# Strided attention of seven batches, two residue classes at a time on the array's rows

## The chip, the cores and the metric

The kernel runs on one core of a Trainium2 chip. The metric is the device time of one execution in microseconds (us). TensorE (PE) multiplies matrices, PEld is its loading of weights, VectorE is DVE, ScalarE is ACT, GpSimd is POOL, and SyncE (SP) issues transfers. All five work from queues of their own, each in the order written, and wait for one another by semaphores.

## The reference

The inputs are q, k and v, each 8 batches x 8 heads x 576 positions x 64 elements. Heads 0 to 3 attend locally, heads 4 to 7 with a stride of 32. The output of attention goes through a two-layer network whose activation is the square of a ReLU.

```python
rel = pos[:, None] - pos[None, :]
mask_local = (rel >= 0) & (rel < 32)
mask_strided = (rel >= 0) & (pos[None, :] % 32 == pos[:, None] % 32)
scores = where(mask, q @ k.T / 8, -1e9)          # mask_local for h < 4, else mask_strided
x = softmax(scores) @ v                          # to 4608 tokens x 512
out = square(maximum(x @ w_in, 0)) @ w_out       # 512 -> 2048 -> 512
```

In a strided head a position attends only to positions of its own residue class modulo 32. There are 32 classes of 18 positions in each head.

## The kernel before, in words

Tokens pass through the network in nine chunks of 512. `mm1(c, ff)` makes one of 16 blocks of the hidden layer of chunk c: four matmuls of 128x512 (L604), a ReLU on ScalarE into one of four `r` buffers (L610), and a square on VectorE into `g_sb` (L611). `mm2` makes the output rows, four such matmuls a group (L626), and ScalarE copies a finished bank out (L630). So the whole run is 288 groups of four wide matmuls each, 32 groups for a chunk: 16 of mm1, then 16 of mm2. Bank `ph` has two buffers.

Attention is woven between these groups. A batch is four units of two heads; units 4b and 4b+1 are local, 4b+2 and 4b+3 strided. Batch 0 comes first (the string `BATCH0`), since chunk 0 needs it. For the others the string `PLAN` gives, for each group number, the words that are run ahead of that group; the numbers are called steps below. What a word issues stands in that order in the queue of each engine it uses, so a late instruction holds up whatever is written behind it on its engine. Work that was put off with `later` is issued at the end of a step. Attention tiles use five PSUM banks named `pt` in rotation.

The words that matter here:

| word | what it does |
|---|---|
| `l`, `c`, `T` | load local q or k rows, cast them into order (`c12kv`: unit 12, k, on VectorE; `a` is ScalarE), transpose them by TensorE (`T12ka`) and copy the result out |
| `r`, `W` | load strided q or k of batch 1 as rows, transpose them by TensorE |
| `C`, `X` | load strided q or k of later batches, transpose them by a transfer of SP |
| `Q`, `Y` | the same for local units of later batches |
| `V`, `U` | load v of the local heads, of the strided heads |
| `o` | load a quarter of `w_out` |
| `S` | scores of a unit, exponentials, masks (the masks come one to four steps later); with `!` the exponentials are issued at once |
| `D`, `E` | local: times v, division, transposition into `xt` |
| `B` | spread a strided unit's v into `vs`, beside columns of ones |
| `F` | strided: times v, one half (`F6.1`: unit 6, odd residues) |
| `z` | constants, at step 0 |

Strided attention before: 72 partitions hold 4 residue classes of 18 positions, so a unit has 8 blocks of 72x72 scores for each of its two heads. `step_S` computes them with 16 matmuls that use half of the array's rows each (one head on rows 0 to 63, the other on 64 to 127, L452), four exponentials of 72x288 (L462) and two masks (L468). `step_X` multiplies by v with 8 matmuls for each half, whose 128 weight columns are v and ones, so that sums come out beside the products (L562). Then come two logarithms (L563), an exponential of minus that (L564), and two multiplications on VectorE that write every second token of `xt` (L567).

Transfers of GpSimd go through one queue of transfers, which is served in order. Eight of them can be under way: before each further one GpSimd waits for the one eight places back. A transfer's descriptors are written when GpSimd issues it.

Of the kernel before, what the change touches and what calls it, by code (L numbers as in the profile page):

```python
# [8 lines left out]
FP32 = mybir.dt.float32  # L9
# [9 lines left out]
    c0qv c0ka T0qa c1kg w2 T0kv S0 c1qv W0k0a w3 W0q0v W0k1a W0q1v T1qv w2 T1kv S2 S1 H0v D0.0 D0.1 S3  # L19
# [4 lines left out]
1: r1q U1  # L24
3: o0
4: r1k c4kv V1 c5qv
5: o1 l2k8+9 c4qv U2
6: o2 o3 V2 C2q
7: C2k
10: l2q8+9 W1q0v T4qa T4kv c5ka T5qa  # L30
12: S4
13: T5ka
14: W1q1v B7v
16: W1k0a S5!
17: W1k1a
18: D4.0
19: S6!
20: D4.1
21: D5.0
22: B6v l3k12+13 S7!  # L40
23: D5.1
24: E5v F7.0
26: X2k l3q12+13
27: E4v F6.0 c9kv
28: F6.1 V3
29: F7.1 c8qv
30: c8ka c9qv
31: X2q
32: U3
# [6 lines left out]
44: S9! D8.0  # L56
46: D8.1
47: E8
48: D9.0 Q16k S10
49: B10v  # L60
50: Q17q Q16q
51: S11! D9.1
52: Q17k
54: F10.0 X3q
55: E9 X3k C4k F10.1 C4q
56: c12qa c13qa
57: c12kv T12ka
58: c13kv B11v V4 T13qv T12qa
59: T13ka
60: F11.0  # L70
61: F11.1
# [3 lines left out]
66: Y17  # L75
67: Y16 D12.1 S13! X4k C5q
68: C5k
71: S14! E12 Q20k Q21q Q20q
72: Q21k
73: D13.0 D13.1  # L80
75: E13 B14v
77: S15
80: F14.0
83: F14.1
86: B15v
89: F15.0
91: S16!
93: F15.1
# [7 lines left out]
103: C6q S18  # L96
104: Y21
105: D17.0
106: Q25k
108: S19 D17.1  # L100
109: Q24k Q24q
111: E17
113: B18v
116: F18.0
119: F18.1
124: V6
125: B19v F19.0 F19.1
# [4 lines left out]
135: E20 X6q S22! C7q Q28k  # L112
137: C7k Q28q Y25 S23
138: D21.0
139: Q29k Q29q D21.1
142: E21
146: B23a B22v
148: F22.0
149: F22.1
151: F23.0  # L120
155: S24!
156: V7 F23.1
# [3 lines left out]
165: S26 D24.1  # L126
167: X7q
171: X7k
172: B26v
173: Y28  # L130
174: E24 D25.0 D25.1
175: F26.0 Y29
178: E25
179: S27!
180: B27v
182: F27.0
186: F26.1 F27.1
191: S28!
192: S29
197: S30!  # L140
198: D28.0
199: D29.0 B30v
200: D28.1 E28
202: S31
204: D29.1
206: E29
209: F30.0
212: B31a
213: F30.1
216: F31.0  # L150
219: F31.1
# [3 lines left out]
def kernel(  # L155
# [9 lines left out]
    nc = tc.nc  # L165
# [13 lines left out]
    SR = 80  # L179

    singles = ctx.enter_context(tc.tile_pool(name="singles", bufs=1))
    qk_st = ctx.enter_context(tc.tile_pool(name="qk_st", bufs=1))
    qk_in = ctx.enter_context(tc.tile_pool(name="qk_in", bufs=4))
    qkT = ctx.enter_context(tc.tile_pool(name="qkT", bufs=4))
    v_st = ctx.enter_context(tc.tile_pool(name="v_st", bufs=2))
# [8 lines left out]
    strT = ctx.enter_context(tc.tile_pool(name="strT", bufs=2))  # L194
# [28 lines left out]
    vss = [singles.tile([SP_, NJ, 3, D], BF16, name=f"vs{i}") for i in range(NV)]  # L223
    str_rows_t = {nm: singles.tile([SR, 4, NJ * D], BF16, name=f"{nm}_t") for nm in "qk"}
# [24 lines left out]
    def load_qk_hw(u):  # L249
        b, p = units[u]  # L250
        s = st.setdefault(u, {})
        for name, src in (("q", q), ("k", k)):
            t = qk_st.tile([QL, 2, 6 * D], FP32, name=f"{name}_st")
            nc.sync.dma_start(out=t, in_=src[b, 2 * p:2 * p + 2].rearrange("h (p j) d -> p h (j d)", j=6))
            s[name + "f"] = t
# [31 lines left out]
    def load_str_rows(b, name):  # L287
        src = q if name == "q" else k
        if b == 0:
            c = 4 if name == "q" else 8  # L290
            t = w_out_b[0:QL, c:c + NP3, :]
        else:
            t = xt[1 if name == "q" else 2][0:QL, T - NP3 * 512:T].rearrange("p (s c) -> p s c", s=NP3)
        nc.gpsimd.dma_start(out=t, in_=src[b, 4:8].rearrange("h (p j) d -> (h p) (j d)", j=NJ)
                            .rearrange("(s p) c -> p s c", p=QL))
        str_rows[b, name] = t

    def step_TS(b, name, g, copy):
        src = str_rows[b, name]
        pt = bank("pt").bitcast(BF16)[:, 0:S]  # L300
        for i in range(2):
            for s3 in range(NP3):
                c = 128 * (2 * g + i)
                o = S // 2 * i + QL * s3
                nc.tensor.transpose(pt[:, o:o + QL], src[:, s3, c:c + 128], ident[0:QL, 0:QL])  # L305
        if g == 0:
            o = strT.tile([128, 2 * NJ * SR], BF16, name=f"{name}T_s")
            str_T[b, name] = o[:, 0:2 * NJ * SP_].rearrange("c (a r) -> c a r", a=NJ // 2)
        o = str_T[b, name]
        copy(o[:, 2 * g:2 * g + 2, :].rearrange("c a r -> c (a r)"), pt)  # L310
        if g == 1:
            for i in range(2):
                st.setdefault(4 * b + 2 + i, {})[name + "T"] = \
                    o[:, :, 2 * SP_ * i:2 * SP_ * (i + 1)].rearrange("c a (h p) -> c h a p", h=2)
# [5 lines left out]
    def load_str_tall(b, name):  # L320
        src = q if name == "q" else k
        t = str_rows_t[name]
        nc.gpsimd.dma_start(out=t[0:SP_], in_=src[b, 4:8].rearrange("h (p j) d -> p h (j d)", j=NJ))  # L323
        big[b, name] = t

    def transpose_str(b, name):
        o = strT.tile([128, 2 * NJ * SR], BF16, name=f"{name}T_s").rearrange("c (n p) -> c n p", p=SR)
        nc.sync.dma_start_transpose(out=o, in_=big.pop((b, name)).rearrange("p h c -> p (h c)"))
        for i in range(2):
            st.setdefault(4 * b + 2 + i, {})[name + "T"] = \  # L330
                o[:, NJ * i:NJ * (i + 1), 0:SP_].rearrange("c (h a) p -> c h a p", h=2)
# [16 lines left out]

    def load_v_str(b):
        t = v_st.tile([SP_, 4, NJ * D], BF16, name="v_st")  # L350
        nc.gpsimd.dma_start(out=t, in_=v[b, 4:8].rearrange("h (p j) d -> p h (j d)", j=NJ))
        for i in range(2):
            st.setdefault(4 * b + 2 + i, {})["vf"] = t[:, 2 * i:2 * i + 2]

    def spread_v_str(u, copy):
        t = vss[v_slot(u)]
        copy(t[:, :, 0:3:2, :], st[u]["vf"].rearrange("p h (j d) -> p j h d", d=D))
        st[u]["v"] = t
# [127 lines left out]

    def load_v0():
        load_v_local_sw(0)
        nc.gpsimd.dma_start(
            out=vs0.rearrange("p u n d -> p (u n d)").rearrange("p (h c) -> p h c", h=4),  # L490
            in_=v[0, 4:8].rearrange("h (p j) d -> p h (j d)", j=NJ))
# [56 lines left out]

    def step_X(u, part):
        run_due(lambda x: x[1] == u)  # L550
        e = st[u]["e"]
        b, p = units[u]
        hw, vt = S // 2, st[u]["v"].rearrange("p j k d -> p j (k d)")
        rv = rv_pool.tile([128, hw], FP32, name="rv")
        pos = []
        for h in range(2):
            po = bank("pt")
            pos.append(po)
            for t in range(NJ // 2):
                w = vt[:, 2 * t + part, D * h:D * (h + 2)]  # L560
                c = S * part + hw * h + SP_ * t
                nc.tensor.matmul(po[:, SP_ * t:SP_ * (t + 1)], w, e[0:SP_, c:c + SP_], start=True, stop=True)  # L562
            nc.scalar.activation(rv[64 * h:64 * h + 64], po[64 - 64 * h:128 - 64 * h, 0:hw], AF.Ln)  # L563
        nc.scalar.activation(rv, rv, AF.Exp, scale=-1.0)  # L564
        for h in range(2):
            r = slice(64 * h, 64 * h + 64)
            nc.vector.tensor_tensor(  # L567
                xt[p][r, b * S:(b + 1) * S].rearrange("c (p j r) -> c p j r", j=NJ // 2, r=2)[:, :, :, part],
                pos[h][r, 0:hw].rearrange("c (j p) -> c p j", p=SP_),
                rv[r].rearrange("c (j p) -> c p j", p=SP_), op=ALU.mult)  # L570
        if part:
            st.pop(u)
# [97 lines left out]
    def run_step(word):  # L670
# [15 lines left out]
        elif op == "F":  # L686
            step_X(int(arg[:-2]), int(arg[-1]))
# [5 lines left out]
        elif op == "P":  # L693
            first_part([int(x) for x in arg])
        elif op == "H":
            shift_v_local(int(arg[:-1]), ENG[arg[-1]])
        elif op == "C":
            load_str_tall(int(arg[:-1]), arg[-1])
        elif op == "Q":
            load_qk_rows(int(arg[:-1]), arg[-1])  # L700
        elif op == "X":
            transpose_str(int(arg[:-1]), arg[-1])
        elif op == "Y":
            transpose_local(int(arg))
        elif op == "V":
            load_v_local_all(int(arg))
        elif op == "U":
            load_v_str(int(arg))
        elif op == "B":
            spread_v_str(int(arg[:-1]), ENG[arg[-1]])  # L710
        elif op == "l":
            load_qk_local_sw(int(arg[0]), [int(x) for x in arg[2:].split("+")], arg[1])
        elif op == "r":
            load_str_rows(int(arg[0]), arg[1])
        elif op == "i":
            load_w_in(int(arg))
        elif op == "o":
            load_w_out(int(arg))
        elif op == "z":
            late_constants()  # L720
        else:
            raise ValueError(word)

    def late_constants():
        nc.vector.tensor_copy(mask_all, mask_loc.to_broadcast([128, NL, QL]))
        nc.vector.memset(mask_all[0:32, 0], 0.0)
        for t in str_rows_t.values():
            nc.vector.memset(t[64:SR], 0.0)
        for t in kTl[2:]:
            nc.vector.memset(t[:, 0:32], 0.0)  # L730
        for t in vss:
            nc.vector.memset(t[:, :, 1, :], 1.0)  # L732
        for i, e in enumerate(es):
            if i > 1:
                nc.vector.memset(e[:, 2 * S:1280], 1.0)
# [112 lines left out]
```

## Time and profile before

| | |
|---|---|
| time of three runs | 311.53, 311.87 (median), 313.56 us |
| span of the profiled execution, first to last instruction | 309.8 us |
| PE, PEld busy | 297.7, 147.1 us |
| DVE, ACT, POOL busy | 165.1, 195.6, 65.7 us |
| wide matmuls of mm1 and mm2, from start to start | 0.216 us |
| stretch of batch 0, up to the steady groups | 22.9 us |
| mean transfer rate | 120 GB/s |

The profile is of one execution, and its page gives the span alone, not that execution's own device time. The three times are of other executions of the same program. Busy times overlap. A matmul's record ends when its result is written, so the next one starts before; costs on TensorE are therefore read from start to start.

### The profile page before, as it was taken

The numbers are of one execution on the slowest core, as the hardware profiler recorded it, in microseconds if no ns is written. First come the engines' busy times: TensorE is split into PE (matmuls) and PEld (weight loads), VectorE is DVE, ScalarE is ACT, GpSimd is POOL, SyncE is SP. The second block draws the span as 40 slices with busy tenths as digits, with TensorE's granted clock in tenths as the row PEclk, the third lists the DMA queues.
The fourth block names the chain that finished last, engine by engine and source line by source line (L and its number), as shares of the span: only waits on it lengthen the run. The fifth ranks groups of instructions, "written<-read, shape, count | busy, mean of one in ns | idle before, by whom it ended". The sixth has DMA issues, their size and how long they took to land.

```text
span 309.8 us, 5985 instructions
## 1 busy us (share of the span) xinstructions
PE 297.7 (96%) x2288; PEld 147.1 (47%) x2288; DVE 165.1 (53%) x388; ACT 195.6 (63%) x421; POOL 65.7 (21%) x90
## 2 busy tenths in 40 slices
PE   7987999999899999999999999999999999999996
PEld 2543555445454444444545454445454544444444
DVE  4568765767647763664367554763586334203400
ACT  3774955876877775675488676865777656316611
POOL 8834422006230026047100740000000000000000
PEclk9999999999999999999999999999999999999999
DMA  8999999997999999799996999711101110010012
GB/s 152 190 204 205 190 197 182 156 156 112 177 161 166 142 124 173 161 118 112 161 205 116 119 176 198 136 24 70 68 2 38 68 70 1 34 68 36 0 67 71
DMA packets 97820, 37.23 MB, mean 120 GB/s; under 512 B 78848, under 2 KB 93312, under 8 KB 97792
## 3 DMA queue, kind: packets, MB, share of 16 engines
q0 software_dynamic: 59136, 18.76, 60.0%
q1 hardware_dynamic: 38512, 18.03, 30.2%
q8 instruction: 18, 0.29, 0.4%
q14 instruction: 10, 0.08, 0.1%
q10 hardware_dynamic: 144, 0.07, 0.1%
HBM read 38.08 MB, written 9.44 MB: 153 GB/s over the span
## 4 chain that ended last, share of the span: by engine, by line
PE 87%; DVE 4%; issue 3%; ACT 3%; DMA 2%; POOL 0%; DVEq 0%; ACTq 0%; POOLq 0%
PE ph L604 39%; PE ph L626 34%; PE pt L452 4%; DMA w_out_b<-in_k_dram 2%; PE pt L562 2%; PE pt L539 2%; DVE xt L567 2%; PE pt L412 1%; PE py L626 1%; PE ph L651 1%; PE pt L626 1%; ACT rv L563 1%; DVE vs L732 1%; ACT rv L564 1%; PE pt L305 1%
## 5 line engine op out<-in xcount | busy, mean ns | idle before, releaser
L604 PE MATMUL ph<-xt,w_in_b 128*128 128x512 bf16 x572 | 132.0, 379 | 3.4 <-ACT r L610 2.6
L626 PE MATMUL ph<-w_out_b,g_sb 128*128 128x512 bf16 x528 | 121.5, 379 | 0.0
L610 ACT ACTIVATE r<-ph 128x512 bf16<-128x512 f32 x143 | 85.4, 599 | 35.1 <-PE ph L604 30.2
L611 DVE TENSOR_TENSOR g_sb<-r 128x512 bf16<-128x512 bf16 x144 | 60.4, 423 | 64.9 <-ACT r L610 63.4
L604 PEld LDWEIGHTS <-w_in_b 128*128 128x128 bf16 x576 | 53.4, 98 | 63.6 <-issue 4.9
L626 PEld LDWEIGHTS <-g_sb 128*128 128x128 bf16 x560 | 51.8, 98 | 56.4
L567 DVE TENSOR_TENSOR xt<-pt,rv 64x288 bf16<-64x288 f32 x56 | 35.9, 642 | 42.0 <-ACT rv L564 40.8
L462 ACT ACTIVATE e<-pt 128x288 bf16<-128x288 f32 (+1 forms) x124 | 44.0, 409 | 13.2 <-PE pt L452 13.1
L630 ACT COPY y<-ph 128x512 f32<-128x512 f32 x33 | 19.3, 584 | 39.7 <-PE ph L626 39.7
L563 ACT ACTIVATE rv<-pt 64x288 f32<-64x288 f32 x56 | 22.7, 405 | 12.6 <-PE pt L562 11.5
L545 DVE TENSOR_TENSOR x_l<-pt,rinv 96x384 bf16<-96x384 f32 x30 | 16.6, 554 | 1.0
L468 DVE TENSOR_TENSOR e<-e,mask_all 128x576 bf16<-128x576 bf16 x28 | 12.7, 453 | 5.5 <-ACT e L462 4.8
L323 POOL DMA_DIRECT2D q_t<-in_q_dram x6 | 4.4, 729 | 51.4 <-DMA qT_s<-q_t 35.2
L468 DVE TENSOR_TENSOR e<-e,mask_str 72x576 bf16<-72x576 bf16 x28 | 12.4, 448 | 3.1 <-ACT e L462 3.1
L562 PEld LDWEIGHTS <-vs 72*128 72x128 bf16 x224 | 10.6, 98 | 6.3 <-DVE xt L567 0.5
L564 ACT ACTIVATE rv<-rv 128x288 f32<-128x288 f32 x28 | 12.4, 442 | 0.9
L378 POOL DMA_DIRECT2D vl<-in_v_dram x7 | 10.1, 1442 | 13.3 <-DMA vl<-in_v_dram 6.4
L562 PE MATMUL pt<-e,vs 72*128 72x72 bf16 x224 | 11.7, 196 | 0.4 <-DVE xt L567 0.4
L262 POOL DMA_DIRECT2D k_l<-in_k_dram x16 | 11.7, 734 | 1.8 <-DMA k_t<-in_k_dram 1.5
L262 POOL DMA_DIRECT2D q_l<-in_q_dram x16 | 11.6, 730 | 1.0 <-issue 0.7
L539 PEld LDWEIGHTS <-e 128*128 128x128 bf16 x192 | 9.0, 98 | 5.7 <-issue 0.4
L323 POOL DMA_DIRECT2D k_t<-in_k_dram x6 | 4.4, 730 | 31.5 <-DMA kT_s<-k_t 30.3
(110 smaller groups left out, 173.9 us busy)
## 6 DMA issues: line engine op xcount, KB each, us to landing
out_dram<-y SPq DMA_DIRECT2D x35, 256.0 KB, 4.1
vl<-in_v_dram POOLq DMA_DIRECT2D x7, 384.0 KB, 13.4
w_in_b<-in_moe_w_in_dram POOLq DMA_DIRECT2D x4, 512.0 KB, 12.1
w_out_b<-in_moe_w_out_dram POOLq DMA_DIRECT2D x4, 512.0 KB, 16.8
v_st<-in_v_dram POOLq DMA_DIRECT2D x7, 288.0 KB, 10.8
q_t<-in_q_dram POOLq DMA_DIRECT2D x6, 288.0 KB, 6.1
k_t<-in_k_dram POOLq DMA_DIRECT2D x6, 288.0 KB, 6.6
xt<-in_q_dram POOLq DMA_DIRECT2D x4, 288.0 KB, 15.3
```

Of the source, the lines that this page charges most:

```text
L262: nc.gpsimd.dma_start(out=t[:, :, hh, :], in_=src[b, 2 * p + hh].rearrange("(t p) d -> p t d", p=QL))
L462: nc.scalar.activation(e[0:kn, lo:lo + S // 2], pss[row][half][0:kn, 0:S // 2], AF.Exp, scale=scale)
L468: nc.vector.tensor_tensor(x, x, m, op=ALU.mult)
L545: nc.vector.tensor_tensor(x, po[0:QL, :, 0:D], rinv[0:QL].to_broadcast([QL, NL, D]), op=ALU.mult)
L562: nc.tensor.matmul(po[:, SP_ * t:SP_ * (t + 1)], w, e[0:SP_, c:c + SP_], start=True, stop=True)
L563: nc.scalar.activation(rv[64 * h:64 * h + 64], po[64 - 64 * h:128 - 64 * h, 0:hw], AF.Ln)
L567: nc.vector.tensor_tensor(xt[p][r, b * S:(b + 1) * S].rearrange("c (p j r) -> c p j r", j=NJ // 2, r=2)[:, :, :, part], pos[h][r, 0:hw].re ...
L604: nc.tensor.matmul(ph, w_in_b[:, kk, 128 * ff:128 * (ff + 1)], xt[kk][:, 512 * c:512 * (c + 1)], start=(kk == order[0]), stop=(kk == order ...
L610: nc.scalar.activation(r, ph, AF.Relu)
L611: later(1, lambda: nc.vector.tensor_tensor(g[:, ff, :], r, r, op=ALU.mult))
L626: nc.tensor.matmul(py, g[:, ff, 128 * j:128 * (j + 1)], w_out_b[:, ff, :], start=(ff == 0), stop=(ff == 15))
L630: nc.scalar.copy(y, py)
```

## The change

Batch 0 and all local attention stay. In batches 1 to 7 the strided part is laid out anew.

Rows of q, k and v are now (head, m) with all 32 residues side by side: 72 rows of 2048 elements. A transposition of 128 columns of them gives two residue classes, the even one on rows 0 to 63 and the odd one on rows 64 to 127. Heads 4, 5 and 6 together have 54 positions of a class. `step_K` copies k so that the even class fills rows 0 to 63 and columns 0 to 53 of a weight tile, and the odd class rows 64 to 127 and columns 64 to 117, with zeros elsewhere; so one matmul of 54 columns computes both classes. The fourth strided head is taken in groups of three classes; that makes 22 weight tiles a batch, 16 + 6. `spread_v_str` spreads v in the same manner. Sums come from one matmul with block-diagonal ones. The 22 tiles are worked off in three parts of 8, 8 and 6: word `s` (scores, one exponential, one mask) and word `x` (sums, products, one logarithm, one exponential, 6, 6 and 4 multiplications into `xt`). Word `k` is `step_K` for one parity and `B` the spread of v for one parity, two each a batch.

The weight tiles must be zero around the blocks. Word `m` sets them, and the spare rows of the transposed transfers, to zero: `mk1v` in batch 0, `mv1g` and `mrg` on GpSimd at steps 1 and 5, `mk0v` and `mv0v` on VectorE at steps 8 and 13. `z` loses its memsets of `vs`, `e`, and of those spare rows, and gains the ones and the mask of the new layout, two selects on GpSimd among them. There is one buffer for the transposed k and for loaded v where there were two, and v of a batch comes in two transfers.

```diff
-5: o1 l2k8+9 c4qv U2
+5: o1 l2k8+9 c4qv mrg
+8: mk0v
-16: W1k0a S5!
+16: W1k0a S5! B10v
-18: D4.0
-19: S6!
-20: D4.1
-21: D5.0
-22: B6v l3k12+13 S7!
+18: D4.0 k10v
+19: k11v
+20: D4.1 s1.0 B11v
+21: D5.0 s1.1 U2
+22: l3k12+13 s1.2
-24: E5v F7.0
+24: E5v x1.0
-27: E4v F6.0 c9kv
+27: E4v x1.1 c9kv
-28: F6.1 V3
-29: F7.1 c8qv
+28: V3
+29: x1.2 c8qv
...
-44: S9! D8.0
-46: D8.1
+44: S9! D8.0 B20v
+45: B21v
+46: D8.1 k20v U3
-47: E8
-48: D9.0 Q16k S10
+47: E8 k21v
+48: D9.0 Q16k s2.0
...
-54: F10.0 X3q
-55: E9 X3k C4k F10.1 C4q
-56: c12qa c13qa
+54: x2.0 X3q
+55: E9 X3k C4k C4q
+56: c12qa c13qa x2.1
 57: c12kv T12ka
...
-60: F11.0
-61: F11.1
+60: x2.2 B30v
+61: B31v
...
+    def step_K(b, par, copy):
+        o = str_T[b, "k"]
+        r = slice(64 * par, 64 * par + 64)
+        kb = kbds[b % 2][r, :, 64 * par:64 * par + W3]
+        copy(kb[:, 0:NP2], o[r, 0:NP2, 0:W3])
+        src = o[r, :, W3:SP_]
+        src = bass.AP(src.tensor, src.offset, [src.ap[0], [SR, NG + 1], [NG * SR, 3], [1, NA]])
+        copy(kb[:, NP2:NB].rearrange("c n (g m) -> c n g m", g=3), src)
...
+    def step_SS(b, part):
+        kb, o = kbds[b % 2], str_T[b, "q"]
+        e = es[2 + b % 2][:, NJ * W3 * part:]
+        ps = bank("pt")
+        n = len(blocks(part))
+        for i, t in enumerate(blocks(part)):
+            rhs = o[:, t, 0:W3] if t < NP2 else three(o, t - NP2)
+            nc.tensor.matmul(ps[:, W3 * i:W3 * (i + 1)], kb[:, t, :], rhs, start=True, stop=True)
+        nc.scalar.activation(e[:, 0:W3 * n], ps[:, 0:W3 * n], AF.Exp, scale=scale)
+        x = e[:, 0:W3 * n].rearrange("p (t c) -> p t c", c=W3)
+        later(1, lambda: nc.vector.tensor_tensor(x, x, mask_bd.to_broadcast([128, n, W3]), op=ALU.mult),
+              (b, part))
+
+    def step_XX(b, part):
...
+        nc.tensor.matmul(pn, ones_bd, e, start=True, stop=True)
+        for i, t in enumerate(blocks(part)):
+            c = slice(W3 * i, W3 * (i + 1))
+            nc.tensor.matmul(po[:, c], vb[:, t, :], e[:, c], start=True, stop=True)
+        rv = rv_pool.tile([128, NJ * W3], FP32, name="rv")[:, 0:W3 * n]
+        nc.scalar.activation(rv, pn, AF.Ln)
+        nc.scalar.activation(rv, rv, AF.Exp, scale=-1.0)
+        for h in (3,) if part == 2 else range(3):
+            for par in range(2):
...
+                    nc.vector.tensor_tensor(to[:, :, NJ * part:NJ * (part + 1), par], of, by, op=ALU.mult)
...
     def late_constants():
...
-        for t in str_rows_t.values():
-            nc.vector.memset(t[64:SR], 0.0)
...
-        for t in vss:
-            nc.vector.memset(t[:, :, 1, :], 1.0)
...
+        nc.vector.memset(ones_bd, 0.0)
+        nc.vector.memset(mask_bd, 1.0)
...
+        nc.gpsimd.affine_select(out=m3, in_=m3, compare_op=ALU.is_ge, fill=0.0,
+                                base=0, channel_multiplier=1, pattern=[[-NA, 3], [0, NA]])
...
+        nc.vector.tensor_copy(mask_bd[64:128], mask_bd[0:64])
```

Here W3 is 54, SR 80, SP_ 72, NA 18, NG 5, NP2 16, NB 22 and NJ 8. The later batches are placed in the plan in the same manner.

## The prediction

> **What bounds the kernel now.** First the page: TensorE is busy for 96% of the span and makes 87% of the chain that ended last. Whatever shortens TensorE's own row of work is gained, and whatever makes it wait is paid in full.
>
> ```profile
> PE 297.7 (96%) x2288; PEld 147.1 (47%) x2288; DVE 165.1 (53%) x388; ACT 195.6 (63%) x421; POOL 65.7 (21%) x90
> PE 87%; DVE 4%; issue 3%; ACT 3%; DMA 2%; POOL 0%; DVEq 0%; ACTq 0%; POOLq 0%
> ```
>
> Then TensorE's timeline, for what strided attention costs between the wide matmuls (start, length, row; starts count, since lengths overlap).
>
> ```profile
> 101.14 0.47 PE L452 MATMUL pt<-qT_s,kT_s 64*72 64x72 bf16 x16
> 101.54 1.90 PE L604 MATMUL ph<-xt,w_in_b 128*128 128x512 bf16 x8
> ...
> 110.19 0.42 PE L562 MATMUL pt<-e,vs 72*128 72x72 bf16 x8
> 110.45 2.76 PE L626 MATMUL ph<-w_out_b,g_sb 128*128 128x512 bf16 x12
> ```
>
> Eight L562 matmuls take 0.26 us, 32.4 ns each. The 16 half-array ones of L452 run in pairs of 36 ns, but the wide matmul before them needs 0.309 instead of 0.216 us and the last pair 0.13: 0.494 us in all per unit.
>
> Last, TensorE's own waits. After batch 0 four are long: 2.46 us (2.30 idle) at 30.51, 0.67 at 54, 1.65 at 85.10, 0.79 at 92. All end with VectorE. The first is the block of constants, step `z`:
>
> ```profile
> 24.90 0.91 DVE L728 MEMSET q_t<- 16x1024 uint32 x1 [0.27 <-issue]
> ...
> 27.10 2.11 DVE L732 MEMSET vs<- 72x512 bf16 x4
> ...
> 29.69 0.34 DVE L281 COPY k_l<-xt 96x768 bf16<-96x768 bf16 x1
> ...
> 30.51 1.02 PE L604 MATMUL ph<-xt,w_in_b 128*128 128x512 bf16 x4 [2.30 <-ACT r L610]
> ...
> 33.06 0.74 DVE L419 COPY kTl<-pt 128x576 bf16<-128x576 bf16 x1
> ...
> 34.22 0.43 PE L452 MATMUL pt<-qT,kTl 64*128 64x96 bf16 x12
> ```
>
> The third stands where `c12kv` waits its turn on VectorE and the transposes `T12ka` wait for it:
>
> ```profile
> 82.01 2.65 DVE L567 TENSOR_TENSOR xt<-pt,rv 64x288 bf16<-64x288 f32 x4 [2.12 <-ACT rv L564]
> ...
> 83.22 0.57 ACT L630 COPY y<-ph 128x512 f32<-128x512 f32 x1
> 83.68 1.56 ACT L281 COPY q_l<-xt 96x768 bf16<-96x768 bf16 x2
> ...
> 84.69 0.62 DVE L281 COPY k_l<-xt 96x768 bf16<-96x768 bf16 x2
> ...
> 85.10 0.43 PE L412 MATMUL pt<-ident,k_l 96*128 96x96 bf16 x6 [1.49 <-DVE k_l L281]
> ```
>
> **The change, part by part.**
>
> *TensorE's work.* Before, a batch costs 2 units of 0.494 and 4 L562 groups of 0.259: 2.02 us. After, it has 44 matmuls of 54 columns with 128x128 weights and 3 of 432, 432 and 324 columns. No row has 54 columns. The rows with weights per matmul go 30.1 ns (65 columns, L539), 32.4 (72), 42.7 (96): 0.406 ns a column, so 25.6 ns for 54. Bounds: 30.1 if the weights set it, 22.5 by 512 columns in 216 ns. The long ones take 0.42 ns a column, 0.50 us. Sum 1.13 + 0.50 = 1.63; saved 0.39 a batch, over 7 batches **-2.8 us** (-1.4 to -3.7). The Trainium skill ("TensorE: Matmul & The Clock Gate", back-to-back issue gap) gives a stream of weight loads and matmuls about 81 ns each at 128 columns; the last rows of this trace (L651) have 128 columns in 56 ns with weights each time, so the measurement decides; by the page's 81 ns the 44 would cost 3.6 us a batch and this term would be +14 us, which the rows refute.
>
> *ScalarE.* 20 activations a batch (8.2 us by 402, 405 and 442 ns) become 9 (about 4.6). Nothing: ScalarE is 63% busy and TensorE sets the end; where its order matters it is counted below.
>
> *VectorE.* Removed a batch: 4 masks of 0.45, 8 writes of 0.64 (L567), 2 v spreads of 0.46: 7.9 us. Added: masks of 432, 432, 324 columns (0.16 + 0.52 ns a column, from 512 in 423 and 576 in 453 ns): 1.1; v spreads of 1408 elements 0.52 each; k spreads, 4 copies. A bf16 copy goes 0.16 us + 0.26 ns an element (L281, L357), so 0.38 and 0.24 us a pair; without that rate 1.05 and 0.49. Writes: 12 of 64x144; L567's 0.64 for 288 makes them 0.33 to 0.41, taken at 0.39, 2.3 us for the six of one part; part 2 about 1.6. Some 10 us a batch. On the average that is hidden (VectorE goes from 53% to about 57%), but not in three places.
>
> *1. Constants.* `z` loses 1.8 us of q_t/k_t memsets (to GpSimd), 2.1 of vs and 0.3 of e; it gains four short memsets and a copy that waits for two GpSimd selects (0.25 each). z ends near 25.9 instead of 29.5 and the wait of 2.46 goes. But VectorE's next work is `c4kv`, and by the record of transfers its input (l1k) lands only at 28.33. From c4k to the end of the kTl copy VectorE took 29.69 to 33.80, 4.1 us; now it starts at 28.38 and a memset of 1408 words stands between (`mk0v`; 0.06 us + 0.83 ns a word from L728 and L742: 1.23), so the copy ends at 33.7 and S4, which reads it, starts at 33.8, not 34.22. Gain **-0.4** (-1.8 if mk0v were free; +0.5). `mk1v` falls into VectorE's idle 2.46 us before 9.71: nothing; without cover 1.2. `mv0v` delays only squares, with four r buffers: nothing.
>
> GpSimd: the selects wait for z's memset at 25.0, and behind them stand r1q, U1, o0, r1k, V1, issued before at 12.59 to 22.11. The queue is served in order and is 14 to 17 us deep (l1k issued 11.92, lands 28.33; r1q follows at 29.23), so r1q issued at 25.7 is in time; with U1's two transfers and the vb memset (1408 words at 1.05 ns by the ident memset, 0.22 us for 128: 1.6) o0 goes at 30, before v lands at 31.15. Nothing; were the memset twice as long, 0.5. `mrg`, 2 x 1.2 us, comes before o2 and o3, whose queue is as deep (2.4 if it were empty). U2 and U3 move later; their single buffer makes them wait for the v spreads, and the k transposes of SP now wait for the k spreads; what they bring is used over 10 us after it landed before; past that, each us late is paid.
>
> *2. k spreads of batch 2* (steps 46, 47), then s2.0 at 48. VectorE is back to back from 70.66 there:
>
> ```profile
> 70.88 0.55 DVE L545 TENSOR_TENSOR x_l<-pt,rinv 96x384 bf16<-96x384 f32 x1
> 71.36 0.44 DVE L468 TENSOR_TENSOR e<-e,mask_all 128x576 bf16<-128x576 bf16 x1
> ...
> 73.29 0.56 DVE L545 TENSOR_TENSOR x_l<-pt,rinv 96x384 bf16<-96x384 f32 x1
> 73.76 0.41 DVE L611 TENSOR_TENSOR g_sb<-r 128x512 bf16<-128x512 bf16 x1
> ```
>
> The plan puts both v spreads (2 x 0.45 from start to start, less 0.22 that VectorE idles before a square at 72.02) and k20 (0.46) ahead of the square at 73.76, and k21's first copy after it: 73.76 + 0.68 + 0.46 + 0.34 + 0.38 + 0.06 for the signal = 75.7. TensorE is ready at 73.97, after D9.0, which starts at 73.78. Wait **+1.7** (to +3.2 at the slow copy rate). Queued behind on TensorE is all of chunk 1's mm2.
>
> *3. T12ka* (step 57). Let P be the start of the first part at step 54 (80.33 before). There TensorE reached T12ka at P + 3.12 and waited until P + 4.77. Now x2.1 stands at step 56, and on ScalarE behind the y copy and both q casts, in the rows above 0.57 and 1.56 us: y at P + 2.3, casts to 4.4, Ln and Exp of 432 columns (0.53 + 0.56) to 5.5. Then six writes (2.3) to 7.8, c12kv 0.34, so T12ka at P + 8.2 against readiness at 3.36: a wait of 4.9 instead of 1.65, **+3.2** (+2.0 with writes of 0.2 us; +3.6).
>
> *Small ones.* The wait at 54 goes (-0.67), but x1.2, behind two parts of six writes, ends 0.3 after mm1 of chunk 1 wants it: -0.4. At 92 a bank no longer waits for L567 (-0.79), D12.0 waits 0.2 for masks: -0.6. Likewise -0.3 at 157 and +0.2 at step 179. Together **-1.1**.
>
> Sum: -2.8 - 0.4 + 1.7 + 3.2 - 1.1 = **+0.6** on the span of 309.8. What lies around the span was 2.1 us to the median run, 311.87, which I keep: 312.5.
>
> **Rivals.**
>
> *The clock falls in the long wait* (slower). The first eight matmuls start 427 ns apart, the later ones 216:
>
> ```profile
> 1.26 3.60 PE L661 MATMUL py<-xt 128*128 128x512 bf16 x8 [1.26 <-DVE xt L742]
> ```
>
> So an array that comes from idling runs at half speed for at least 3 us (the granted clock row says 1.00 there, so spacing must tell). The longest later idle time, 2.30 at 30.51, slowed nothing. The wait at T12ka is twice that. If the point lies between, some 3.4 us at half speed cost 1.7, up to twice that if the slow stretch is longer: 312.5 + 2.5 = 315. It decides from an idle time somewhere above 2.3 us. The Trainium skill names one (same page, the HAM clock gate): a free-running window of about 3.4 us of idleness brings half rate. By that rule a wait of 4.9 us holds a whole window in (4.9 - 3.4)/3.4, four cases in ten.
>
> *Copies and weights at the slow ends*: k spreads at 1.05 and 0.49 (+1.5 at s2.0), 54-column matmuls at 30 ns (+1.4), a little more at steps 20 and 64: 316. For it: no copy here has runs of 54 elements. Against: all bf16 copies in SBUF show the fast rate.
>
> *The saving shows* (faster): short writes and spreads near 0.2 us (-1.2, -0.6), 22.5 ns matmuls (-0.9), the wait of 2.46 won whole because l1k lands earlier or mk0v is hidden (-1.4): 308.4. Against: the order on ScalarE alone holds T12ka to P + 7.
>
> **Numbers.** Forecast (312.5, own range 309.5 to 315) 0.5; clock 0.2; slow ends 0.16; saving 0.14. One per cent, about what a measurement of this kernel can tell from no change, is 308.75 and 315.0. Faster: 0.1 from the last case, 0.02 from the forecast's edge: 0.12. Slower: 0.12 of the clock case, 0.12 of the slow ends, 0.06 of the forecast: 0.30. Range 309.0 to 317.5.
>
> **What would show it.** Right: 54-column matmuls 25 to 26 ns apart; no 64-row mode but in local attention; S4 near 33.8; a TensorE wait of 1.5 to 2 us ended by a kb copy, and one near 5 us ended by k_l in L295. Rival: wide matmuls 427 ns apart after that one. Wrong: T12ka waiting under 3 us, or waits of over 1 us that are not named here.

## The result, and the profile after

The changed kernel takes 345.23 us (median of 4 runs, 344.35 to 345.97), the kernel before 311.90 (4 runs, 311.53 to 313.56) on the same chip: a ratio of 1.103, interval 1.097 to 1.110. The forecast was 312.5, with a range up to 317.5. Three executions measured for the next section stand far from the others of their kernel (319.06 us with the homes exchanged, 344.41 with r1q alone moved, 1077.71 of the kernel before) and enter no ratio. The profiled execution took 344.35 with a span of 342.6; before, the span was 309.8.

From the page after: TensorE's share, its busy tenths in 40 slices of 8.6 us, the clock granted in the same slices, and the chain that ended last.

```profile
PE 299.2 (87%) x2177; PEld 148.0 (43%) x2177; DVE 181.3 (53%) x467; ACT 173.2 (51%) x342; POOL 70.0 (20%) x102
...
PE   6984001999997499999999999999999999999996
...
PEclk9998555899999879999999999999999999999999
...
PE 78%; DMA 8%; DVE 5%; POOL 4%; ACT 2%; issue 2%; DVEq 0%; POOLq 0%
```

TensorE's busy time is about what it was (297.7 before); its share fell from 96% to 87%, and two slices are all but empty. The loss is a wait, and transfers make 8% of the chain, 2% before. The granted clock reads 0.5 where TensorE stands and 0.7 in one slice near 120 us. The timeline of that stretch (start, length, engine, row, idle time before it and what ended it):

```profile
25.37 0.23 POOL L793 TENSOR_SCALAR_AFFINE_SELECT mask_bd<-mask_bd 64x54 bf16<-64x54 bf16 x1 [12.30 <-DVE mask_bd L789]
...
25.90 0.56 POOL L310 DMA_DIRECT2D xt<-in_q_dram  x1
...
29.70 0.55 POOL L310 DMA_DIRECT2D xt<-in_k_dram  x1
...
39.02 0.69 POOL L288 DMA_DIRECT2D xt<-in_k_dram  x1 [6.58 <-DMA xt<-in_k_dram]
...
45.48 0.74 POOL L288 DMA_DIRECT2D xt<-in_q_dram  x1
...
58.95 0.66 PE L319 MATMUL pt<-ident,xt 72*128 72x72 bf16 x8 [29.41 <-DMA xt<-in_q_dram]
...
60.85 1.48 PE L659 MATMUL ph<-xt,w_in_b 128*128 128x512 bf16 x3
```

The two L310 rows are r1q and r1k, the two L288 rows l2k and l2q. By the record of transfers r1q landed at 30.21, r1k at 38.73 and l2q at 58.91. The first transposes of r1q (W1q0, L319), which TensorE reached at 29.4, start 0.04 us after l2q has landed, not after r1q. And l2k was issued 0.3 us after r1k had landed. Behind the wait the wide matmuls stand 427 ns apart, up to 63.0.

The rest of the span is close to what was forecast. TensorE's timeline where nothing waits, strided scores (L535), then sums and outputs (L546, L549):

```profile
136.67 0.36 PE L535 MATMUL pt<-qT_s,kb 128*128 128x54 bf16 x8
136.87 1.02 PE L659 MATMUL ph<-xt,w_in_b 128*128 128x512 bf16 x4
...
145.35 0.35 PE L546 MATMUL pt<-e,ones_bd 128*128 128x432 bf16 x1
145.54 0.38 PE L549 MATMUL pt<-e,vb 128*128 128x54 bf16 x8
145.75 2.75 PE L681 MATMUL ph<-w_out_b,g_sb 128*128 128x512 bf16 x12
```

Eight scores take 0.204 us from the last wide matmul to the next, less its own 216 ns: 25.4 ns each; eight outputs with their long matmul take 0.400, of which the long one has 0.182, so 27.2 ns each. Last, the two waits of batch 2 and batch 3:

```profile
104.78 0.46 DVE L366 COPY kb<-kT_s 64x324 bf16<-64x324 bf16 x1
104.92 0.38 PE L535 MATMUL pt<-qT_s,kb 128*128 128x54 bf16 x8 [1.72 <-DVE kb L363]
...
113.66 1.56 ACT L295 COPY q_l<-xt 96x768 bf16<-96x768 bf16 x2
115.12 0.52 ACT L551 ACTIVATE rv<-pt 128x432 f32<-128x432 f32 x1
...
116.28 2.46 DVE L559 TENSOR_TENSOR xt<-pt,rv 64x144 bf16<-64x144 f32 x6 [1.40 <-ACT rv L552]
...
118.76 0.62 DVE L295 COPY k_l<-xt 96x768 bf16<-96x768 bf16 x2
119.18 0.66 PE L450 MATMUL pt<-ident,k_l 96*128 96x96 bf16 x6 [4.78 <-DVE k_l L295]
119.64 1.91 PE L681 MATMUL ph<-w_out_b,g_sb 128*128 128x512 bf16 x4
```

s2.0 waits for the k spread, T12ka for c12kv behind six short writes of x2.1, these behind Ln and Exp, and these behind the q casts, as forecast. The four wide matmuls in the last row take 1.91 us instead of 1.03.

The terms of the span: W1q0's wait 29.57 and the slow work behind it 1.9; T12ka's wait and slow work 7.55 in place of 1.65; s2.0 1.89; z's wait -2.46; TensorE's own work 7 batches of 2.02 - 1.66, -2.5; the small waits about -1.1. Sum +33.2; measured +32.8.

### The profile page after: what moved, and what is told of

Read it like the earlier page. It is cut to its first block, busy times and chain, and to the rows that moved or that the text cites. A ratio compares the mean times of both kernels' runs of the same rounds, so it can differ in the third digit from the quotient of the medians.

```text
span 342.6 us, 5744 instructions
## 1 busy us (share of the span) xinstructions
PE 299.2 (87%) x2177; PEld 148.0 (43%) x2177; DVE 181.3 (53%) x467; ACT 173.2 (51%) x342; POOL 70.0 (20%) x102
## 4 chain that ended last, share of the span: by engine, by line
PE 78%; DMA 8%; DVE 5%; POOL 4%; ACT 2%; issue 2%; DVEq 0%; POOLq 0%
PE ph L659 34%; PE ph L681 32%; DMA xt<-in_k_dram 4%; DMA xt<-in_q_dram 4%; DVE xt L559 2%; PE pt L490 2%; PE pt L450 2%; PE pt L619 1%; PE pt L535 1%; PE ph L706 1%; PE pt L549 1%; PE pt L546 1%; DVE g_sb L666 1%; PE py L681 1%; POOL w_out_b L426 1%
## 5 line engine op out<-in xcount | busy, mean ns | idle before, releaser
L659 PE MATMUL ph<-xt,w_in_b 128*128 128x512 bf16 x572 | 133.7, 381 | 1.3 <-ACT xt L644 0.8
L559 DVE TENSOR_TENSOR xt<-pt,rv 64x144 bf16<-64x144 f32 x84 | 34.0, 405 | 20.0 <-ACT rv L552 18.9
L500 ACT ACTIVATE e<-pt 128x288 bf16<-128x288 f32 (+1 forms) x68 | 24.0, 417 | 7.7 <-PE pt L490 7.7
L319 PE MATMUL pt<-ident,xt 72*128 72x72 bf16 x32 | 1.9, 210 | 29.4 <-DMA xt<-in_q_dram 29.4
L457 ACT COPY qT<-pt 128x576 bf16<-128x576 bf16 x5 | 3.3, 650 | 31.1 <-PE pt L450 31.1
L551 ACT ACTIVATE rv<-pt 128x432 f32<-128x432 f32 (+1 forms) x21 | 10.5, 501 | 14.5 <-PE pt L546 14.5
L565 DVE TENSOR_TENSOR xt<-pt,rv 64x270 bf16<-64x270 f32 (+1 forms) x28 | 10.9, 432 | 10.9 <-ACT rv L552 10.8
L319 PEld LDWEIGHTS <-xt 72*128 72x128 bf16 x32 | 1.7, 106 | 30.6 <-DMA xt<-in_q_dram 29.9
L536 ACT ACTIVATE e<-pt 128x432 bf16<-128x432 f32 (+1 forms) x21 | 10.4, 497 | 8.1 <-PE pt L535 7.6
L388 POOL DMA_DIRECT2D v_st<-in_v_dram x7 | 3.7, 530 | 47.0 <-DVE vb L395 46.8
```

The lines of the kernel that those rows point to most:

```text
L500: nc.scalar.activation(e[0:kn, lo:lo + S // 2], pss[row][half][0:kn, 0:S // 2], AF.Exp, scale=scale)
L551: nc.scalar.activation(rv, pn, AF.Ln)
L559: nc.vector.tensor_tensor(to[:, :, NJ * part:NJ * (part + 1), par], of, by, op=ALU.mult)
L565: nc.vector.tensor_tensor(t, of[:, g:, :, lo:lo + k], by[:, g:, :, lo:lo + k], op=ALU.mult)
L659: nc.tensor.matmul(ph, w_in_b[:, kk, 128 * ff:128 * (ff + 1)], xt[kk][:, 512 * c:512 * (c + 1)], start=(kk == order[0]), stop=(kk == order ...
```

## The experiments

Ratios in this section are to the kernel before as it ran beside the variants, with medians of 313.0 to 313.4 us.

**Where the wait comes from.** The theory after reading the trace: two loads share scratch columns. `load_str_rows` now puts r1q and r1k in the last 2048 columns of xt[1] and xt[0], 2560 to 4607; `load_qk_local_sw` puts l2q and l2k in columns 1536 to 3071 of the same two tiles. Before, r1 took 1536 columns from 3072 on, and r1k lay in xt[2]. So 512 columns overlap. The plan names l2q (step 10) ahead of W1q0, so in program order the last writer of 512 columns that W1q0 reads is l2q: it waits for l2q. l2k (step 5) may not write before r1k has landed, and on GpSimd mrg, o2, o3, V2, C2q, C2k and l2q stand behind it. The rivals: GpSimd's late issue alone, or dearer matmuls.

The same order says what W1q0 reads. The 512 columns hold the first eight residue classes of r1q, and l2q has landed in them, at 58.91, when W1q0 starts. In the changed kernel these classes of batch 1 thus get q from rows of batch 2's local heads. Likewise k: l2k landed at 45.17, and W1k0 comes after 58.95. So the overlap costs time and also changes what is computed.

*The homes exchanged.* l2 goes to columns 3072 to 4607 of xt[3] and xt[2], l3 to those of xt[1] and xt[0].

```diff
-            c = T - 6 * D * ((4 if name == "k" else 2) if b == 0 else 4 if b == 3 else 8)
-            i = (0 if name == "k" else 1) if b == 2 else 2 if b and name == "k" else 3
+            c = T - 6 * D * ((4 if name == "k" else 2) if b == 0 else 8 if b == 1 else 4)
+            i = (0 if name == "k" else 1) if b == 3 else 2 if b and name == "k" else 3
```

> The changed kernel with the scratch places of batch 2's and batch 3's local loads exchanged: l2q and l2k go to columns 3072 to 4607 of xt[3] and xt[2], l3q and l3k to those of xt[1] and xt[0]. So l2q no longer writes 512 of the columns that r1q has filled and W1q0 reads, nor l2k those of r1k. Theory (the overlap alone made the change slow): TensorE's wait of 29.6 us at 58.95 goes, and with it the slow matmuls behind it (the whole stretch cost 30.4 us more than its 26 transposes should, and about 1.1 more in wide matmuls at 427 ns). 345.2 - 31.5 = 313.7; up to 0.7 more if W1q0 now waits for r1q, which lands at 30.2: 313 to 315. The waits of 1.9 us (s2.0) and 4.9 us (T12ka) stay as they were. Rival A (GpSimd's queue, held by the two selects until 25.4, makes every load late): another TensorE wait of over 2 us appears before 60 us and the time is 316 to 325. Rival B (the block-diagonal matmuls cost much more than counted): no new wait, but the time stays above 320.

Measured: 314.39 us (11 runs), 1.004 of before, interval 1.001 to 1.008. TensorE's waits (total, times, longest), then rows of the timeline:

```profile
PE pt L450 <- DVE k_l L295: 4.8, 1, 4.8
PE pt L535 <- DVE kb L363: 1.7, 1, 1.7
...
PE pt L319 <- DMA xt<-in_q_dram: 0.6, 1, 0.6
```

```profile
32.19 0.43 PE L319 MATMUL pt<-ident,xt 72*128 72x72 bf16 x8 [0.58 <-DMA xt<-in_q_dram]
...
34.37 0.74 POOL L288 DMA_DIRECT2D xt<-in_k_dram  x1
...
36.06 0.43 PE L490 MATMUL pt<-qT,kTl 64*128 64x96 bf16 x12 [0.94 <-DVE kTl L457]
```

W1q0's wait is 0.6 us, now for r1q, and l2k no longer waits in GpSimd's queue. The two lines that place l2 and l3 are worth 30.8 us, and with them W1q0 and W1k0 read what r1q and r1k loaded. Both rivals fall as causes of the 30 us.

*The order instead of the place*: the columns overlap, but l2q stands behind W1q1 and l2k behind W1k1.

```diff
-5: o1 l2k8+9 c4qv mrg
+5: o1 c4qv mrg
-10: l2q8+9 W1q0v T4qa T4kv c5ka T5qa
+10: W1q0v T4qa T4kv c5ka T5qa
-14: W1q1v
+14: W1q1v l2q8+9
-17: W1k1a
+17: W1k1a l2k8+9
```

> The changed kernel with its own scratch places, but with l2q issued after W1q1 (step 14) and l2k after W1k1 (step 17): the columns still overlap, but now the load waits for the reader and not the reader for the load. Overlap theory: the wait of 29.6 us goes here too; l2q and l2k then land about 15 us after TensorE passes step 17 (near 37 us), near 52 us, and T8kv at step 35 is due at about 53: 313.5 to 317. If GpSimd's late issue and not the overlap were the cause, this order, which issues the two loads later still, would be slower than 320.

Measured: 318.60 (2 runs), a little over the range.

```profile
59.66 0.36 DVE L295 COPY k_l<-xt 96x768 bf16<-96x768 bf16 x1 [1.72 <-DMA xt<-in_k_dram]
```

```profile
PE ph L659 <- DVE xt L565: 1.9, 1, 1.9
```

The 29.6 us are gone here too, so the order of reader and load decides. What was under-sized: l2k landed at 59.57, not near 52, and c9kv, which stands ahead of x1.2's writes on VectorE, waited 1.72 us for it; so chunk 1's first mm1 waited 2.11 us from start to start instead of 0.42. That is 1.7 of the 4.2 us by which it stands over the variant before; the cause of the rest stays open.

*The kernel before with the overlap alone.*

```diff
+            if b == 2 and name == "q":
+                c += 512
```

> The kernel before with one edit: l2q moved up by 512 columns in xt[1], so that it writes 512 of the columns that r1q has filled and W1q0 reads (W1q0 and W1q1 then transpose l2q's values there). Nothing else of the change is in it. Overlap theory: W1q0, which ran at 31.37 us, has to wait for l2q's landing at about 56.7 us (it is issued at 41.49 behind six other loads and cannot come much earlier): a wait of 24 to 26 us, then some 2 us of slow clock: 337 to 340. If what slowed the change lies in its new instructions, this stays at 312.

Measured: 337.38 (2 runs), ratio 1.081, interval 1.074 to 1.087. TensorE's timeline and, first, GpSimd's issue of l2q:

```profile
40.12 0.69 POOL L276 DMA_DIRECT2D xt<-in_q_dram  x1 [2.02 <-DMA w_out_b<-in_moe_w_out_dram]
```

```profile
55.10 0.66 PE L307 MATMUL pt<-ident,xt 96*128 96x96 bf16 x6 [23.72 <-DMA xt<-in_q_dram]
...
57.00 3.42 PE L606 MATMUL ph<-xt,w_in_b 128*128 128x512 bf16 x8
```

None of the block-diagonal form is in this kernel, and it has the wait, with eight matmuls in 3.42 us behind it. That the overlap suffices is shown from both sides.

*Only the keys' overlap left* (l2q as in the first variant, l2k as in the change).

```diff
+            if b in (2, 3) and name == "q":
+                i, c = (3 if b == 2 else 1), T - 1536
```

> The changed kernel with only the queries' overlap removed (l2q in xt[3], l3q in xt[1], columns 3072 to 4607); l2k still writes 512 of the columns that r1k has filled and W1k0 reads. Overlap theory: W1q0 no longer waits for l2q; l2k still stands in GpSimd's queue until r1k has landed (38.7) and lands near 45, so W1k0, ready near 38.5, waits about 6.5 us, with some 1.5 to 2 of slow matmuls: 313 + 8 = 319 to 323. If the query's overlap were all, 313 to 315.

Measured: 323.50 (2 runs), a little over the expected 319 to 323.

```profile
PE pt L321 <- DMA xt<-in_k_dram: 6.2, 1, 6.2
PE pt L452 <- DVE k_l L297: 4.8, 1, 4.8
```

The keys' overlap costs 9.1 us by itself, a wait of 6.2 and slow matmuls. In the change it costs TensorE nothing where it stands, since W1k0 comes after the longer wait for l2q. That it makes that wait longer, by holding GpSimd's queue, is not seen: l2q landed at 58.91 in the change, and at 60.02 (homes exchanged) and 57.61 (the reordered variant below) where l2k did not wait.

**The waits of s2.0 and T12ka.**

```diff
-44: S9! D8.0 B20v
-45: B21v
-46: D8.1 k20v U3
-47: E8 k21v
+44: S9! D8.0
+45: k20v
+46: D8.1 k21v
+47: E8
...
-49: s2.1
-50: Q17q Q16q s2.2
+49: s2.1 B20v
+50: B21v Q17q Q16q s2.2 U3
...
-56: c12qa c13qa x2.1
-57: c12kv T12ka
-58: c13kv V4 T13qv T12qa
+56: c12kv c13kv c12qa c13qa x2.1
+57: T12ka
+58: V4 T13qv T12qa
```

> The first variant (exchanged places) with two reorderings on VectorE: c12kv and c13kv at step 56 ahead of x2.1, and batch 2's k spreads at steps 45 and 46 ahead of the v spreads, which go to 49 and 50 (U3 after them). Theory (the two waits were made by the order on VectorE, and the first one's clock loss goes with it): T12ka waits under 1 us instead of 4.9 and the matmuls behind it start 216 ns apart, s2.0 waits under 0.5 instead of 1.9. Against the first variant -4.5 -1.5 (slow matmuls) -1.6 = about -7.5: 305 to 308, faster than before. Rival: the waits only move, to T13ka or to x2.0 behind the later v spreads, and 309 to 313 is left.

Measured: 307.04 (4 runs), 0.985 of before, interval 0.980 to 0.989, and 7.35 us under the variant with the homes alone.

```profile
74.02 0.38 PE L535 MATMUL pt<-qT_s,kb 128*128 128x54 bf16 x8 [0.63 <-DVE kb L363]
...
84.43 0.43 PE L450 MATMUL pt<-ident,k_l 96*128 96x96 bf16 x6 [0.93 <-DVE k_l L295]
84.70 1.03 PE L681 MATMUL ph<-w_out_b,g_sb 128*128 128x512 bf16 x4
```

From start to start the waits left are 0.79 and 1.09 us, a little over what was expected; they were 1.89 and 4.94. Four matmuls take 1.03 us again. The order on VectorE had made both waits, as forecast. This is the reordered variant that the following sections speak of.

**What is left in the order.** Two variants go on from there. The first moves r1q alone ahead of z:

```diff
-0: l1q4+5 l1k4+5 z
-1: r1q U1 mv1g
+0: l1q4+5 l1k4+5 r1q z
+1: U1 mv1g
```

with mk0v at step 32, c9kv at 29 behind x1.2, both k spreads at 45, and c12kv and c13kv at 54.

> The variant with exchanged places, with all the waits attacked that its trace and that of the reordered one still show: r1q issued ahead of z (W1q0 waited 1.41 us for it), mk0v from step 8 to 32 (the kTl copy that S4 waits for stood 1.2 us behind it: 0.63), c9kv behind x1.2's writes (0.42 at the first mm1 of chunk 1), k20 and k21 both at step 45 (s2.0 waited 0.79), c12kv and c13kv at step 54 ahead of x2.0, where VectorE idles for 3.15 us (T12ka waited 1.09). Theory (each of these waits is the order on one engine): -1.4 -0.5 -0.4 -0.6 -1.0 = -3.9 on 307.0: 302.5 to 304. Rival (order has nothing more to give; what goes at one place comes back at the next): 305 to 307.

Measured: 308.56 us (3 runs, 306.03 to 310.18), 0.982 of before, interval 0.971 to 0.993: outside both ranges that were expected, not better than the last one, and too scattered to say by how much worse. In its profile W1q0's wait is gone, but U1, still behind the selects, was issued at 28.11 (batch 0 had slow matmuls there: step z starts at 26.86, in the variant before at 24.29), and what stands behind it came late:

```profile
PE ph L681 <- DMA w_out_b<-in_moe_w_out_dram: 1.2, 1, 1.2
PE pt L619 <- DMA vl<-in_v_dram: 1.2, 1, 1.2
```

The second moves the selects instead (`f` on GpSimd behind V1, `g`, VectorE's copy, at step 19), with mk0v, c9kv and the k spreads as in the first, and leaves c12kv and c13kv at step 56:

```diff
-4: r1k c4kv V1 c5qv
+4: r1k c4kv V1 f c5qv
-19: k11v
+19: k11v g
```

> The reordered variant again (exchanged places, c12kv and c13kv at step 56), with the two selects for the mask moved on GpSimd from step 0 to behind V1 at step 4, and VectorE's copy of the mask to step 19, so that r1q, U1, o0 and r1k no longer stand behind VectorE's constants; mk0v at step 32, c9kv behind x1.2, k20 and k21 at step 45. In the reordered variant l1k landed at 27.4 and the next load, r1q, at 30.4: 3.0 us for a transfer that took 0.9 before, so about 2 us in which the queue was empty. Theory (the selects held up the loads): r1q is issued near 13 us and lands near 28.5, the loads behind it 1.5 to 2 us earlier than in the reordered variant, W1q0 does not wait (-1.4), S4 -0.5, x1.2 -0.4, s2.0 -0.5: 303 to 305. Rival (the waits come back at the next place, as they did in the variant with r1q alone moved, where V1 and o1 were late): 306 to 308.

Measured: 306.47 us (6 runs), 0.979 of before, interval 0.975 to 0.984. That is in the rival's range. Against the 307.04 it is no certain gain; it is the lowest median of this study. GpSimd's queue now:

```profile
13.08 0.56 POOL L310 DMA_DIRECT2D xt<-in_q_dram  x1
15.24 0.54 POOL L388 DMA_DIRECT2D v_st<-in_v_dram  x1 [1.60 <-DMA g_sb<-in_v_dram]
...
22.76 0.53 POOL L310 DMA_DIRECT2D xt<-in_k_dram  x1 [2.01 <-DMA w_in_b<-in_moe_w_in_dram]
```

W1q0 and W1k0 do not wait there. The profiled execution has slow matmuls in batch 0 (last section), an estimated 2.2 us that are not the variant's: its step z starts at 26.52, in the reordered variant at 24.29.

**The kernel before with the same care.** z keeps mask_all and kTl; its other memsets go to steps of their own (`nr`: q_t and k_t, `n0` to `n3`: vs, `ne`: e). Then also c12kv and c13kv at step 54.

```diff
-14: W1q1v B7v
+2: nr
+9: n3 ne
+14: W1q1v B7v
+15: n2
-24: E5v F7.0
+24: E5v F7.0 n0 n1
```

> The kernel before with the block of constants of step z spread: the memsets of q_t and k_t at step 2, of vs at steps 9, 15 and 24, of e at step 9. No part of the block-diagonal form is in it. Theory: TensorE's wait of 2.46 us at 30.51 goes, S4 starts 1.4 to 2.2 us earlier, and no idle time over 1.7 us is left after batch 0, so the granted clock is 0.998 or more in every run (the kernel before had 0.989 to 0.995 in 18 of 31 runs, which are 1.7 to 3.5 us slower): 309.5 to 310.3. Rival for the clock: it has nothing to do with the 2.3 us, and about half of the runs have 0.995 or less again.

Measured: 310.33 us (8 runs), 0.991 of before, interval 0.988 to 0.994, and some 1.5 us under those runs of the kernel before that had the full clock (last section); S4 starts at 32.23 instead of 34.22, and 7 of 8 runs have a granted clock of 1.00.

```diff
-54: F10.0 X3q
+54: c12kv c13kv F10.0 X3q
-57: c12kv T12ka
+57: T12ka
-58: c13kv B11v V4 T13qv T12qa
+58: B11v V4 T13qv T12qa
```

> The same with c12kv and c13kv moved to step 54, ahead of F10.0, so that T12ka does not wait 1.65 us for them. Theory: 1.3 to 1.6 us less than the variant with the constants spread: 308 to 309. That is what the kernel before gives with the same care for VectorE's order; what the block-diagonal form is worth on TensorE is then the difference to the reordered variants of the changed kernel, 2.5 us by the sum of its matmuls. If the form gives more through the work that it takes from ScalarE, the difference is 4 us or more.

Measured: 309.56 us (4 runs), 0.988 of before, interval 0.984 to 0.992: above the range of 308 to 309. The rows of T12ka with the constants spread, and then of T12ka and T12qa with both moves:

```profile
83.14 0.43 PE L415 MATMUL pt<-ident,k_l 96*128 96x96 bf16 x6 [1.50 <-DVE k_l L284]
```

```profile
82.66 0.42 PE L415 MATMUL pt<-ident,k_l 96*128 96x96 bf16 x6
...
84.52 0.68 PE L415 MATMUL pt<-ident,q_l 96*128 96x96 bf16 x12 [0.57 <-ACT q_l L284]
```

T12ka's wait, 1.66 us from start to start after the first move, is gone after the second; but now the transposes of q behind it wait 0.74 us for ScalarE's cast. So the second move brought 0.8 us and not 1.3. The best version of the change is 3.1 us under this, near the 2.5 that its matmuls alone should bring; as the two orders were not tuned alike, that is no clean measure of the form.

**The clock.** Six or ten idle memsets ahead of c12kv lengthen T12ka's wait in the reordered variant.

> The reordered variant (exchanged places, c12kv and c13kv at step 56, k spreads first) with six idle memsets of 256 words ahead of c12kv on VectorE, 0.27 us each: T12ka's wait grows from 1.09 to about 2.7 us. Theory 1 (the clock falls only from an idle time of a whole window, some 3.4 us as a rule): matmuls behind it stay 216 ns apart, time 307.0 + 1.6 = 308.6, granted clock 1.00 in every run. Theory 2 (it depends on where the idle time falls, and may fall from less than a window): in part of the runs a clock of 0.99 and about 1.2 to 1.7 us more.

> The same with ten memsets: T12ka's wait about 3.8 us. Theory 1: (3.8 - 3.4) / 3.4, one run in ten, has a clock under 1.00; time 307.0 + 2.7 = 309.7. Theory 2: most or all runs have a clock of 0.99, and the time is 311 to 311.5. (The wait of 4.94 us gave a clock of 0.989 or 0.994 in each of the runs of the variant that has it, where theory 1 expects it in four or five of ten.)

```diff
-56: c12kv c13kv c12qa c13qa x2.1
+56: d6 c12kv c13kv c12qa c13qa x2.1
...
+        elif op == "d":
+            for _ in range(int(arg)):
+                nc.vector.memset(pad, 0.0)
```

The memsets took 0.38 us each, not 0.27, so the waits became 3.3 and 4.9 us instead of 2.7 and 3.8. Measured: 312.24 (10 runs) and 314.39 (10 runs), by 5.2 and 7.4 us over the variant without them, where the waits grew by 2.2 and 3.8. The first one's profile:

```profile
86.81 0.61 PE L451 MATMUL pt<-ident,k_l 96*128 96x96 bf16 x6 [3.16 <-DVE k_l L296]
87.23 1.05 PE L682 MATMUL ph<-w_out_b,g_sb 128*128 128x512 bf16 x2
...
89.89 1.24 PE L682 MATMUL ph<-w_out_b,g_sb 128*128 128x512 bf16 x4
```

The wide matmuls behind the wait are 427 ns apart until 90.3. A clock under 0.996 was granted in 7 of 10 runs of the first and in all of the second: theory 2 in kind, at a higher price than it named. The fall is not all of the 5.2: the three runs with the full clock took 310.64 to 313.31. What a wait of 2.7 us would do stays open, since the first missed that length.

## Why the prediction was wrong

The step that failed is the one on GpSimd: "r1q issued at 25.7 is in time", "Nothing". It asked when r1q is issued and lands, and not who else writes where it lands. The new shape of `load_str_rows` was costed as a transfer; its columns were not set against those of l2q and l2k, which the diff does not touch. That omission is 30.8 of the 32.7 us between the forecast and the result (345.23 to 314.39).

Even its own question was answered 0.7 to 1.4 us too well. r1q was issued at 25.90, as forecast, but landed at 30.21, not with the queue at 29.23: l1k had landed at 27.69 and the queue had run dry. With the queue filled earlier (last variant) the wait is gone.

Point by point, the other steps:

- TensorE's work, forecast 1.63 us a batch: 1.66 (three groups of scores 0.204, 0.204 and 0.154, of outputs 0.400, 0.400 and 0.301). 25.6 ns a matmul was forecast; the scores took 25.4, the outputs 27.2, outside the "25 to 26" named as a sign (and the lower bound, 512 columns in 216 ns, is 22.8 and not 22.5). The term is right to 0.2 us over seven batches.
- Constants: S4 was forecast at 33.8 and starts at 33.83 in the reordered variant, whose profile has no slow matmuls after the first eight. It waits 0.63 us for the kTl copy, which mk0v holds up. The path is right; the number is so by luck, as shown below the list.
- s2.0, +1.7: 1.89 us, as the kb copy that it waits for took 0.46 us instead of 0.24. T12ka, a wait of 4.9: 4.94. x1.2, 0.4: 0.42. All ended by the named copies. Right.
- The small ones: z's wait and the two at 54 and 92 are gone; of the 0.2 at D12.0 and at step 179 nothing is seen, no wait after 125 us reaches 0.3.
- The clock rival came true, and it was underrated. It was given 0.2; in every run of the variant with the homes exchanged the granted clock was under 0.996, and in its profile the matmuls behind T12ka stand 427 ns apart. Its 314.39 lies where that rival was put (315). The Trainium skill ("TensorE: Matmul & The Clock Gate", Part 1) says that half rate comes after an idle window of about 3.4 us, and that the window is free-running. The four cases in ten that the prediction made of it were too few, by these runs.
- The rival of slow ends and that of the short writes: the copies of a kb pair mostly took 0.38 and 0.23 us, six writes 2.46 to 2.53 (2.3 forecast). Neither.

The luck in S4 shows in these rows of the reordered variant:

```profile
27.26 1.31 POOL L805 MEMSET vb<- 128x1408 f32 x1
27.39 1.40 DVE L295 COPY k_l<-xt 96x768 bf16<-96x768 bf16 x1 [1.18 <-DMA xt<-in_k_dram]
...
33.83 0.43 PE L490 MATMUL pt<-qT,kTl 64*128 64x96 bf16 x12 [0.46 <-DVE kTl L457]
```

l1k landed at 27.36, not 28.33, so c4kv began 1.0 us early; but it took 1.40 us, not 0.34, beside the memset of mv1g on GpSimd. The prediction had counted that memset in GpSimd's queue alone. The two errors cancel.

With the overlap away the kernel takes 314.39, inside the forecast's own range, and the sum's 312.5 lacks the fallen clock and r1q's 0.6 us. The other terms were right to a few tenths, that of the constants by luck; one wait was not in the sum.

On l2k's wait of 6.58 us for r1k: the Trainium skill ("DMA: Bandwidth & Descriptors", Two DMAs through the same engine are not ordered) says that two transfers on one queue are not ordered by it, and that the issuing engine has to be made to wait for the first one's completion. The trace has that wait: GpSimd stood until 0.3 us after r1k had landed, with six loads behind it. What would come without it no run here shows.

## What to carry to other kernels

When a load changes shape or home, list every tile and column range that it shares with other loads, and for each reader ask which write to its columns comes last in program order: a wait for a load that the reader does not need looks, in the trace, like a late transfer of the right tensor, and the reader then gets that load's data. Match the wait's end with the landing of each load into that tile before blaming the queue. In a queue served in order, keep instructions that wait for another engine behind the loads that others wait for, and fix the order on the engines before judging a new form by its time.

## What the runs showed of the hardware

The clock falls after shorter idle times than the prediction took. Counting the runs whose granted clock was under 0.996, by the longest idle time of TensorE after batch 0 in the kernel's profile: up to 1.5 us (five variants) 2 of 25; 2.3 us (the kernel before, in the three later comparisons) 28 of 46; 3.2 us 7 of 10; 4.7 to 4.8 us (three variants) 22 of 22. In the kernel before, the runs with the lower clock take some 1.8 us more (medians 313.6 and 311.8), which is most of the spread of its times; with z's block spread, 7 of 8 runs had the full clock. So "2.30 at 30.51 slowed nothing" holds for the profiled execution only. The counts tie the fall to the wait by kernel, not by run: where the clock fell is seen in profiled executions alone, and in that of the ten memsets it fell once more in batch 0, where wide matmuls stand 427 ns apart up to 23.1 us. The Trainium skill ("TensorE: Matmul & The Clock Gate", Part 1, table of the two states) gives half rate after at least one idle window of about 3.4 us. As a need for a whole idle window that does not fit the counts at 2.3 us; that the outcome differs from run to run fits the free-running window of the same part.

The start differs too. Two profiles, the variant with the homes exchanged and the reordered one, same two matmuls in batch 0:

```profile
5.88 1.05 PE L716 MATMUL py<-xt 128*128 128x512 bf16 x2
```

```profile
5.71 0.60 PE L716 MATMUL py<-xt 128*128 128x512 bf16 x2
```

In the first, wide matmuls go on starting 427 ns apart until 13.6 us, in the second until 4.2. W1q0 stands 1.75 us later in the first, although it waited 0.7 us less. The granted clock's row shows nothing of it, the spacing does; and the order in batch 0 is the same in both. The Trainium skill (same page and part) says that the number of slow matmuls at a kernel's start differs from run to run with the window's phase. The traces agree: 14 wide ones have records of over 0.6 us in the first, 8 in the second.

A memset on GpSimd held up bf16 copies on VectorE. In all eight profiles in which a cast of c4 or c5 overlaps mv1g's memset (1.3 us), the cast ends 0.2 us after the memset and takes 0.58 to 2.04 us. In the last variant of the change, where the memset comes earlier, c4kv takes 0.36 us, and the memset runs beside products from PSUM that keep their 0.55 us.
